# Scores over 64 rows, TensorE operands at multiples of 64 bytes, query weights in quarters of 128 columns

## The chip, the cores and the metric

The kernel runs on one core of one Trainium2 chip. The metric is the device time of one execution in microseconds, as the median of three runs. TensorE is called PE, its load of the stationary operand PEld, VectorE DVE, ScalarE ACT, GpSimd POOL and SyncE SP, as in the profile. "Stationary" is the operand of a matmul that is loaded into the array first, "moving" the one that streams through it.

## What is computed

One transformer block over 2048 tokens of width 576. Attention has 32 query heads of width 18 and one head of keys and values that all of them share; the feed-forward part multiplies two linear branches and has no other nonlinearity.

```python
# x: [1, 2048, 576], H = 32, Dh = 18, F = 4608
q = (ln(x) @ wq), in 32 heads of 18;  k = ln(x) @ wk;  v = ln(x) @ wv
p = softmax(q k^T * 18 ** -0.5)
h = x + (p v, heads side by side) @ wo
g, u = ln(h) @ w_gate, ln(h) @ w_up
out = h + (g * u) @ w_down
```

## The kernel before

**Tiling.** The tokens are worked on in four blocks of 512 (`TB`), the keys in 16 tiles of 128. Attention of a block goes over 8 groups of four heads, over 16 key tiles, and over two pairs of heads. `pair` (L573) does one such step: `scores` (L591) issues two matmuls, one for each head of the pair. One has its operands in partitions 0 and up, the other in partitions 64 and up, so that each uses half of the array's rows. Then ACT takes the exponential of both, 128x1024 values, in one instruction (L594). The operands of a score have 56 rows: 54 of them are 18 query rows in a split of three parts, and rows 54 and 55 hold a bound of the score that is subtracted (the keys' rows there are -1). `flush` and `values` (L596) multiply the exponentials with the values: four matmuls of 32 columns each, in float32, which the trace shows as eight.

**Precision.** Nearly all other matmuls are in the type float32r, and each product of two matrices is done in three passes, high by high, high by low and low by high, with the halves made by a cast and a subtraction (`split`, L86).

**Feed-forward.** `ffn(b)` (L966) goes over 36 slices of 128 hidden columns. A slice is a sweep of 27 steps; each step is a pair of matmuls over 64 rows (L986), one for the gate and one for the up branch, in the two halves of the array, with the normalised tokens `X` moving and the weights `ws` stationary. While attention of a later block is still to be done, a sweep calls `pair` ahead of steps 0, 4, 8, ..., 24 (L983), and the results go to the tiles `pg` and `pu`; in the last block they go to `gu`. Behind every second sweep `down` (L892) multiplies two slices with the down weights: 42 matmuls (L946) of 128 rows, 128 columns and 288 moving columns. There the products of gate and up, which lie in the tile `room` as `A`, are the stationary operand, and the weights `wdo` move. The output projection of attention (`project`, L733, matmuls at L750) has the same shape, with its stationary operand in `oT` or in `o_hl`, a part of `room`.

**Order of the work.** Every engine executes its instructions in the order in which the program issues them, and that order is written out by hand: attention of block 0 first, beside the projections of the queries, then attention of blocks 1 to 3 inside the sweeps of blocks 0 to 2, then the sweeps of block 3 alone. In the opening part (`keys_values`, L134) TensorE projects keys, values and the queries of block 0 (L233, L284), and turns the normalised tokens (L201, L210). The queries of blocks 1 to 3 are projected in `queries` (L436), as pairs of matmuls over 64 rows and 126 columns, seven heads at a time.

**Query tiles.** The tile of a group's queries has two buffers, taken in turn from a pool (L346, L559). Four DMAs on SP's queue fill it (`load_q`, `load_m`): 54 rows and 2 rows for each half. Partitions 56 to 63 and 120 to 127 are not filled. In the keys, `kT`, the partitions 32 to 63 and 96 to 127 are set to -1 once (L163) and then filled up to row 53 of each half.

**Where tiles lie.** Tiles lie one behind the other in the order of the pools, each rounded up to 32 bytes of a partition. With the sizes in the code, `kT`, `V`, the query tiles, the exponentials, `X`, `ws`, `wdo` and the `XT` of the four blocks start at multiples of 64 bytes. The pool `oT`, which holds `x23`, `oT` and `room` one after the other, starts 32 bytes past one. The query weights `wq_h` and `wq_l` have rows of 504 columns (2016 bytes), and a group of seven heads starts every 504 bytes, so that most of their slices start off a multiple of 64.

Of the kernel before, what the change touches and what calls it, by code (L numbers as in the profile page):

```python
# [17 lines left out]
F32 = mybir.dt.float32  # L18
F32R = mybir.dt.float32r
I32 = mybir.dt.int32  # L20
AF = mybir.ActivationFunctionType
ALU = mybir.AluOpType
# [3 lines left out]
P = 128  # L26
S, D, H, DH, F = 2048, 576, 32, 18, 4608
TB = 512
NB = S // TB
NQ = TB // P  # L30
# [24 lines left out]
class Block:  # L55
# [78 lines left out]
    def keys_values(self, others):  # L134

        pe, act, dve, sp, pool = self.pe, self.act, self.dve, self.sp, self.nc.gpsimd
        p0 = self.op
        x01 = [self.hp.tile([P, NQ, D], F32, tag="h", name=f"x{b}") for b in range(2)]
        x23 = self.otp.tile([P, 2, NQ, D], F32, tag="oT", name="x23")
        xs = x01 + [x23[:, 0], x23[:, 1]]  # L140
        self.h.update(enumerate(x01))
        wkr = self.qp.tile([P, 5, 6 * DH], F32, tag="q", name="wkr")
        cols = [(slice(None), slice(None), slice(h0 * DH, (h0 + n) * DH)) for h0, n in QT]
        wqr = [self.qp.tile([P, 5, 7 * DH], F32, tag="q", name="wqr0")]
        wqr += [self.w0.tile([P, 5, 7 * DH], F32, tag="wo_r", bufs=3, name=f"wqr{i}") for i in range(1, 4)]
        for lo, hi in ((0, 1), (1, 2), (2, 4)):
            sp.dma_start(xs[0][:, lo:hi], self.tokens(self.x, 0)[:, lo:hi])
        sp.dma_start(self.C, self.cst)
# [8 lines left out]
        n = 5 * 6 * DH  # L157
# [17 lines left out]

        def scale(lo, hi, eng):
            r = self.rstd(mv[:, lo:hi, 1], f"a{lo}", eng, hi - lo)
            n = self.lp.tile([P, hi - lo], F32, tag=f"n{hi - lo}", name=f"n{lo}")
            if eng is pool:
                pool.tensor_tensor(n, mv[:, lo:hi, 0], r, ALU.mult)  # L180
                pool.tensor_scalar(n, n, -1.0, None, ALU.mult)
            else:
                dve.scalar_tensor_tensor(n, mv[:, lo:hi, 0], -1.0, r, ALU.mult, ALU.mult)
            for j in range(lo, hi):
                rs[j] = r[:, j - lo:j - lo + 1], n[:, j - lo:j - lo + 1]
# [33 lines left out]
        def parts(n=3):  # L219

            for _ in range(n):
                b, r, tr = trs.pop(0)
                XT = self.XT[b]
                if r is None:
                    self.split_tail(XT[:, 8, :], tr)
                else:
                    sl = slice(2 * r * P, (2 * r + 2) * P)
                    self.split(XT[:, 0:4, sl], XT[:, 4:8, sl], tr)

# [43 lines left out]
            dve.tensor_copy(self.V[:, lo:hi, 1:1 + DH], psv[:, :, 44 - DH:44])  # L273

        def highs(i, cast):
            cast(self.wq_h[cols[i]], wqr[i])

        def lows(i):
            pool.tensor_tensor(self.wq_l[cols[i]], wqr[i], f32(self.wq_h[cols[i]]), ALU.subtract)

        def query(i):
            psq = psqs[i] = self.ps_f(f"psq0_{i}")
            for k, (w, m) in enumerate(highs_first(self.wq_h[cols[i]], self.wq_l[cols[i]], self.XT[0])):
                pe.matmul(psq[:7 * DH], w, m, start=(k == 0), stop=(k == 13))  # L284
                yield

# [15 lines left out]
            self.flush(len(self.pend) - 1)  # L302

        q0, q1, q2, q3 = (query(i) for i in range(4))
        warm = self.ps_a("warm")
        for _ in range(WARM):
            pe.transpose(warm[:, 0:P], self.ident, self.ident)
        stats(0, 4)
# [13 lines left out]
        lows(2)  # L322
        stats(6, 8)
        scale(4, 8, pool)
        drain(project(0))
        mean()
        some(q0, 15)
# [15 lines left out]
        apply(1, 2, 3)  # L343
        stats(10, 11)
        some(q1, 6)
        q = self.qt[0, 0] = self.qp.tile([P, 2, TB], F32R, tag="q", name="q0_0")  # L346
        some(k0)
        self.load_q(q, 0, 0)
        self.load_m(q, 0, 0)
# [86 lines left out]
    def queries(self, b):  # L436

        pe, act, dve, sp = self.pe, self.act, self.dve, self.sp
        for i, (h0, n) in enumerate(QT):
            r = n * DH  # L440
            psq, psr = self.ps_f(f"psq{b}_{i}"), self.ps_f(f"psr{b}_{i}")
            w_h, w_l = self.wq_h[:, :, h0 * DH:h0 * DH + r], self.wq_l[:, :, h0 * DH:h0 * DH + r]
            for k, (w, m) in enumerate(passes(w_h, w_l, self.XT[b])):
                for o, ps in ((0, psq), (64, psr)):
                    pe.matmul(ps[:r], w[o:o + 64], m[o:o + 64], start=(k == 0), stop=(k == 13))
                if k < 13:
                    yield 1
                if k == 5 and self.tqs and 0 < self.tqs[0][0] < b:
                    self.bounds(self.tqs[0][0])
            qs = self.qb.tile([P, 2, TB], F32R, tag="qs", bufs=QS, name=f"qs{b}_{i}")  # L450
            t = f32(qs[:r, 0])
            dve.tensor_copy(t, psr[:r])
            src = f32(qs[:r, 1])
            dve.tensor_tensor(src, psq[:r], t, ALU.add)
            self.parts_q(r, qs, src)
            drain(self.store_q(b, h0, n, qs))
            yield 2.5
        self.last_heads(b)
        yield 0
        if b == NB - 1:  # L460
            yield 4
            self.bounds(b)
# [90 lines left out]
    def prefetch_q(self, b, g):  # L553

        if g == NG:
            b, g = b + 1, 0
        if b == NB or (b, g) in self.qt or self.known[b] < 4 * g + 4:
            return
        self.qt[b, g] = q = self.qp.tile([P, 2, TB], F32R, tag="q", name=f"q{b}_{g}")  # L559
        self.load_q(q, b, g)  # L560
        self.load_m(q, b, g)

# [27 lines left out]

    def scores(self, s_, p_, q, t, pr):  # L591
        for i, o in enumerate((0, 64)):
            self.pe.matmul(s_[:, i], self.kT[o:o + 56, t * P:(t + 1) * P], q[o:o + 56, pr], start=True, stop=True)  # L593
        self.act.activation(p_, s_, AF.Exp, scale=SCALE)  # L594

    def values(self, acc, Ps, t):  # L596
# [114 lines left out]

    def load_wo_0(self, c):

        w = self.w0.tile([P, 5, 7 * DH], F32, tag="wo_r", bufs=3, name=f"wo_r{c}")
        r = self.wo_r0[c] = w.rearrange("p a b -> p (a b)")[:, 0:D]
        self.sp.dma_start(r, self.wo0[:, c])

    def split_wo_0(self):
# [437 lines left out]
    def run(self):  # L1156
# [8 lines left out]
        with ExitStack() as st:  # L1165
            pool = lambda name, bufs, **k: st.enter_context(tc.tile_pool(name=name, bufs=bufs, **k))
            cp, self.lp, self.hp = pool("const", 1), pool("ln", 2), pool("resid", 2)
            self.qp, self.pp, self.op, self.otp = pool("q", 2), pool("P", P_BUFS), pool("o", 1), pool("oT", 1)
            self.ps, self.w0 = pool("ps", 1, space=PSUM), pool("w0", 3)
            self.C = cp.tile([P, C_W], F32, name="C")  # L1170
            self.ident = self.C[:, C_ID:C_ID + P]
            self.kT = cp.tile([P, S], F32R, name="kT")
            self.V = cp.tile([P, NT, 32], F32, name="V")
            self.G = cp.tile([P, 64], F32R, name="G")
            self.mx = cp.tile([H, 8], F32, name="mx")
            st.enter_context(tc.manual_schedule())
            with tc.tile_pool(name="p0q", bufs=1) as self.p0q:
                self.wq_h = self.p0q.tile([P, 5, 28 * DH], F32R, name="wq_h")
                self.wq_l = self.p0q.tile([P, 5, 28 * DH], F32R, name="wq_l")
                self.kvq = self.p0q.tile([P, NB, TB], F32, name="kvq")  # L1180
                self.XT = [self.p0q.tile([P, 9, TB], F32R, tag=f"XT{b}", name=f"XT{b}") for b in range(NB)]
                with tc.tile_pool(name="qb", bufs=2) as self.qb:
                    def rest():
                        for b in range(1, NB):
                            yield from self.queries(b)
                    others = rest()
                    self.keys_values(others)
                    self.cast = self.dve.tensor_copy
                    live, due = True, 0.0
                    while live:  # L1190
                        if self.n_pair >= WO_FROM and not self.wo_r0:
                            for c in range(3):
                                self.load_wo_0(c)
                        self.pair()
                        due += RATE
                        while due > 0 and live:
                            z = next(others, None)
                            live = z is not None
                            due -= z or 0
                        self.pair()  # L1200
                        self.run_aux(1)
                        self.flush(len(self.pend) - 1)
            self.wp, self.hh, self.p2 = pool("w", 2), pool("hid", 4), pool("P2", 1)
            self.blocks()
            self.guard()
# [4 lines left out]
P_BUFS = 6  # L1210
# [34 lines left out]
def f32(ap):  # L1245
    return ap.bitcast(F32)
# [10 lines left out]
def highs_first(W, Wl, XT):  # L1257

    p = passes(W, Wl, XT)
    return p[0:12:3] + p[2:12:3] + p[1:12:3] + p[12:]  # L1260
# [7 lines left out]
def drain(gen):  # L1268
    for _ in gen:
        pass  # L1270
# [76 lines left out]
```

## Time and profile before

| | |
|---|---|
| median of 3 runs | 2292.12 us (2291.93 to 2294.34) |
| profiled execution | 2291.9 us |
| its span, first to last instruction | 2290.4 us |
| granted TensorE clock | 0.999 |
| PE busy | 2268.7 us, 99% |
| ACT, DVE, POOL busy | 1436.5, 1180.3, 681.3 us |

The profiled execution took 1.5 us more than its span, and it lies within the range of the runs. Matmuls are pipelined: one starts while the one before it still runs, so the durations in a row of the profile overlap, and the pace of TensorE is read from the distance of starts. In the view in order of time, a row gives the start of a run of like instructions, the time from its start to its end, the engine, the line and what was done, with the count behind the "x".

### The profile page before, as it was taken

The page shows a single profiled execution, that of the slowest core. Times are in us where ns is not written, and L with a number is a line of the kernel's source. Part 1 is how long each engine was busy: PE and PEld are TensorE (multiplying, and loading weights), DVE is VectorE, ACT ScalarE, POOL GpSimd, SP SyncE. Part 2 cuts the span into 40 slices and gives each one's busy share as a digit, 9 for nine tenths or more (in the row PEclk, how much of TensorE's full clock was granted, in tenths as well). Part 3 has the DMA queues.
Part 4 walks back from the last instruction along what each step waited for, and adds up shares of the span by engine and source line. Part 5 has one row for each costly group of instructions (what it writes and reads, how often), then busy time and mean ns, then how long its engine had stood idle before and what let it go on. Part 6 is the DMA issues. An engine that isn't in the chain of part 4 may idle for free.

```text
span 2290.4 us, 45926 instructions
## 1 busy us (share of the span) xinstructions
PE 2268.7 (99%) x18114; PEld 1599.6 (70%) x18114; DVE 1180.3 (52%) x2152; ACT 1436.5 (63%) x1877; POOL 681.3 (30%) x856
## 2 busy tenths in 40 slices
PE   8999999999999999999999999999999999999998
PEld 6333346677777767677767677777767788888987
DVE  8232435565656567343434355444444476566665
ACT  5889887776676666767666767667677623232332
POOL 4000003455554444122221222222122233333342
PEclk9999999999999999999999999999999999999999
DMA  5222304434333344533333343633333354655553
GB/s 176 81 75 73 111 30 136 148 139 151 136 122 128 136 159 137 207 115 122 113 114 105 125 128 125 192 125 120 98 118 118 120 173 171 213 171 171 179 186 109
DMA packets 127129, 306.75 MB, mean 134 GB/s; under 512 B 17553, under 2 KB 17681, under 8 KB 126265
## 3 DMA queue, kind: packets, MB, share of 16 engines
q1 hardware_dynamic: 126905, 303.73, 39.8%
q8 instruction: 145, 2.38, 0.4%
q14 instruction: 79, 0.65, 0.1%
HBM read 233.76 MB, written 55.67 MB: 126 GB/s over the span
## 4 chain that ended last, share of the span: by engine, by line


## 5 line engine op out<-in xcount | busy, mean ns | idle before, releaser
L594 ACT ACTIVATE P<-s 128x1024 f32<-128x1024 f32 x1024 | 1024.0, 1026 | 271.4 <-PE s L593 189.6
L986 PE MATMUL pg<-X,ws 64*128 64x512 f32 x2592 | 706.9, 391 | 0.0
L986 PE MATMUL pu<-X,ws 64*128 64x512 f32 x2592 | 706.7, 391 | 0.1
L986 PEld LDWEIGHTS pg<-X,ws 64*128 64x128 f32 x2592 | 480.2, 186 | 75.9 <-issue 1.2
L986 PEld LDWEIGHTS pu<-X,ws 64*128 64x128 f32 x2592 | 478.1, 186 | 19.1 <-DVE h L751 1.0
L598 PE MATMUL acc<-P,V 128*32 128x512 f32 x4096 | 487.9, 598 | 0.0
L593 PE MATMUL s<-q,kT 56*128 56x512 f32 x2048 | 455.3, 423 | 5.2 <-ACT P L594 3.3
L946 PEld LDWEIGHTS y<-wdo,room 128*128 128x128 f32 x2856 | 386.9, 188 | 46.7 <-issue 44.2
L946 PE MATMUL y<-wdo,room 128*128 128x288 f32 x2856 | 403.7, 300 | 0.0
L953 ACT COPY tmp<-y 128x288 f32<-128x288 f32 x408 | 162.7, 399 | 330.8 <-PE y L946 313.2
L593 PEld LDWEIGHTS s<-q,kT 56*128 56x128 f32 x2048 | 208.1, 184 | 199.4 <-ACT P L594 118.3
L986 PE MATMUL gu<-X,ws 64*128 64x512 f32 x2592 | 301.8, 389 | 0.5 <-DMA X<-X 0.5
L954 POOL TENSOR_TENSOR x<-x,tmp 128x288 f32<-128x288 f32 x204 | 159.1, 810 | 446.2 <-ACT tmp L953 445.7
L598 PEld LDWEIGHTS acc<-P,V 128*32 128x32 f32 x4096 | 114.0, 109 | 242.5 <-issue 231.1
L986 PEld LDWEIGHTS gu<-X,ws 64*128 64x128 f32 x2592 | 247.6, 184 | 48.8 <-issue 4.8
L88 POOL CAST ws<-wr 128x1152 fp32r<-128x1152 f32 x144 | 170.9, 1187 | 325.6 <-PE pu L986 176.2
L954 POOL TENSOR_TENSOR h<-h,tmp 128x288 f32<-128x288 f32 x204 | 159.1, 810 | 345.8 <-ACT tmp L953 345.6
L89 DVE TENSOR_TENSOR ws<-wr,ws 128x1152 fp32r<-128x1152 f32 x144 | 199.1, 1383 | 74.7 <-POOL ws L88 74.7
L1020 DVE TENSOR_TENSOR hf<-pu,g 128x512 f32<-128x512 f32 x96 | 66.3, 691 | 269.0 <-ACT g L1016 265.6
L949 DVE TENSOR_TENSOR x<-x,y 128x288 f32<-128x288 f32 x272 | 117.7, 452 | 145.6 <-PE y L946 145.6
L949 DVE TENSOR_TENSOR h<-h,y 128x288 f32<-128x288 f32 x272 | 118.4, 454 | 111.8 <-PE y L946 109.8
L89 DVE TENSOR_TENSOR room<-S,room 128x1024 fp32r<-128x1024 f32 x68 | 85.1, 1251 | 147.7 <-ACT room L88 147.7
(172 smaller groups left out, 1621.9 us busy)
## 6 DMA issues: line engine op xcount, KB each, us to landing
wdo<-wd_dram SPq DMA_DIRECT2D x369, 288.0 KB
wr<-in_wgu_dram SPq DMA_DIRECT2D x144, 576.0 KB
wd_dram<-wdo SPq DMA_DIRECT2D x123, 288.0 KB
q<-q_dram SPq DMA_DIRECT2D x64, 216.0 KB
raw<-in_wd_dram SPq DMA_DIRECT2D x36, 288.0 KB
q_dram<-qs SPq DMA_DIRECT2D x15, 504.0 KB
X<-X SPq DMA_DIRECT2D x24, 256.0 KB
ob<-ob SPq DMA_DIRECT2D x121, 36.0 KB
```

Source lines behind the costliest of these rows:

```text
L88: (copy or self.cast)(hi, src)
L89: self.dve.tensor_tensor(lo, src, f32(hi), ALU.subtract)
L593: self.pe.matmul(s_[:, i], self.kT[o:o + 56, t * P:(t + 1) * P], q[o:o + 56, pr], start=True, stop=True)
L594: self.act.activation(p_, s_, AF.Exp, scale=SCALE)
L598: self.pe.matmul(acc[32 * j:32 * j + 32, :], self.V[:, t, :], Ps[j // 2][:, j % 2, :], start=(t == 0), stop=(t == NT - 1), skip_group_chec ...
L946: pe.matmul(y[:, :HD], m[:, t * P:(t + 1) * P], k, start=(first and j == 0), stop=(j == 2), skip_group_check=True)
L949: dve.tensor_tensor(hs, hs, y[:, :HD], ALU.add)
L953: act.copy(z, y[:, :HD])
L954: pool.tensor_tensor(hs, hs, z, ALU.add)
L986: pe.matmul(ps, w[o:o + 64, wk, c], X[o:o + 64, xk, c], start=(j == 0), stop=(j == 26))
L1020: dve.tensor_tensor(hf, pu, g, ALU.mult)
```

## The change

Three things are changed together.

1. **Scores.** Both operands of a score now have 64 rows. Rows 56 to 63 of the keys are -1 already; the queries' rows there must be zero. So there are two query tiles for the whole kernel, `self.q2`, set to zero once by POOL and used in turn, in place of tiles that are taken from the pool for each group.
2. **Places.** A tile of 8 floats, `gap`, goes ahead of `oT` in its pool, and smaller tiles change their size or place (the scale tile `n`, and the raw query weights `wqr`, which now lie where `XT3` comes later), so that `oT`, `room` and what lies behind them start at multiples of 64 bytes. `XT3` is made when it is first written.
3. **Query weights.** `wq_h` and `wq_l` are kept as four quarters of 128 columns, of which 126 are used, so that each slice starts at a multiple of 64 bytes.

The scratch of TensorE's opening transposes (`warm`) moves to another PSUM tile.

```diff
@@ keys_values
+        self.otp.tile([P, 8], F32, tag="gap", name="gap")
         x23 = self.otp.tile([P, 2, NQ, D], F32, tag="oT", name="x23")
-        wkr = self.qp.tile([P, 5, 6 * DH], F32, tag="q", name="wkr")
+        wkr = self.qp.tile([P, 5, 6 * DH], F32, tag="q0", name="wkr")
-        wqr = [self.qp.tile([P, 5, 7 * DH], F32, tag="q", name="wqr0")]
-        wqr += [self.w0.tile([P, 5, 7 * DH], F32, tag="wo_r", bufs=3, name=f"wqr{i}") for i in range(1, 4)]
+        wqr = [self.qp.tile([P, 5, 7 * DH], F32, tag="q1", name="wqr0")]
+        late = self.p0q.tile([P, 3, 5, 7 * DH], F32, tag="XT3", name="wqr")
+        wqr += [late[:, i] for i in range(3)]
...
-            n = self.lp.tile([P, hi - lo], F32, tag=f"n{hi - lo}", name=f"n{lo}")
+            n = self.lp.tile([P, NQ], F32, tag="n", name=f"n{lo}")[:, :hi - lo]
...
+                if b == len(self.XT):
+                    self.XT.append(self.p0q.tile([P, 9, TB], F32R, tag=f"XT{b}", name=f"XT{b}"))
...
-            cast(self.wq_h[cols[i]], wqr[i])
+            cast(self.wq_h[:, :, i, :7 * DH], wqr[i])
...
-        warm = self.ps_a("warm")
+        warm = self.ps_m("warm")
...
         scale(4, 8, pool)
+        self.q2 = [self.qp.tile([P, 2, TB], F32R, tag=f"q{i}", name=f"q{i}") for i in range(2)]
+        for q in self.q2:
+            pool.memset(f32(q), 0.0)
...
-        q = self.qt[0, 0] = self.qp.tile([P, 2, TB], F32R, tag="q", name="q0_0")
+        q = self.qt[0, 0] = self.q2[0]
@@ queries
-            w_h, w_l = self.wq_h[:, :, h0 * DH:h0 * DH + r], self.wq_l[:, :, h0 * DH:h0 * DH + r]
+            w_h, w_l = self.wq_h[:, :, i, :r], self.wq_l[:, :, i, :r]
@@ prefetch_q
-        self.qt[b, g] = q = self.qp.tile([P, 2, TB], F32R, tag="q", name=f"q{b}_{g}")
+        self.qt[b, g] = q = self.q2[g % 2]
@@ scores
-            self.pe.matmul(s_[:, i], self.kT[o:o + 56, t * P:(t + 1) * P], q[o:o + 56, pr], start=True, stop=True)
+            self.pe.matmul(s_[:, i], self.kT[o:o + 64, t * P:(t + 1) * P], q[o:o + 64, pr], start=True, stop=True)
@@ load_wo_0
-        w = self.w0.tile([P, 5, 7 * DH], F32, tag="wo_r", bufs=3, name=f"wo_r{c}")
-        r = self.wo_r0[c] = w.rearrange("p a b -> p (a b)")[:, 0:D]
+        r = self.wo_r0[c] = self.w0.tile([P, D], F32, tag="wo_r", bufs=3, name=f"wo_r{c}")
@@ run
-                self.wq_h = self.p0q.tile([P, 5, 28 * DH], F32R, name="wq_h")
-                self.wq_l = self.p0q.tile([P, 5, 28 * DH], F32R, name="wq_l")
+                self.wq_h = self.p0q.tile([P, 5, 4, P], F32R, name="wq_h")
+                self.wq_l = self.p0q.tile([P, 5, 4, P], F32R, name="wq_l")
-                self.XT = [... for b in range(NB)]
+                self.XT = [... for b in range(NB - 1)]
```

The code of the lows (`wq_l`) and of `query` is changed as that of the highs. The number, shape and order of the matmuls and of the exponentials stay, but for the 64 rows.

More of the change, by code (lines that the diff above doesn't have):

```diff
@@ L275, in highs @@
         def highs(i, cast):
-            cast(self.wq_h[cols[i]], wqr[i])
+            cast(self.wq_h[:, :, i, :7 * DH], wqr[i])
         def lows(i):
-            pool.tensor_tensor(self.wq_l[cols[i]], wqr[i], f32(self.wq_h[cols[i]]), ALU.subtract)
+            pool.tensor_tensor(self.wq_l[:, :, i, :7 * DH], wqr[i], f32(self.wq_h[:, :, i, :7 * DH]), ALU.subtract)
         def query(i):
             psq = psqs[i] = self.ps_f(f"psq0_{i}")
-            for k, (w, m) in enumerate(highs_first(self.wq_h[cols[i]], self.wq_l[cols[i]], self.XT[0])):
+            for k, (w, m) in enumerate(highs_first(self.wq_h[:, :, i, :7 * DH], self.wq_l[:, :, i, :7 * DH], self.XT[0])):
                 pe.matmul(psq[:7 * DH], w, m, start=(k == 0), stop=(k == 13))
@@ L1167, in run @@
             cp, self.lp, self.hp = pool("const", 1), pool("ln", 2), pool("resid", 2)
-            self.qp, self.pp, self.op, self.otp = pool("q", 2), pool("P", P_BUFS), pool("o", 1), pool("oT", 1)
+            self.qp, self.pp, self.op, self.otp = pool("q", 1), pool("P", P_BUFS), pool("o", 1), pool("oT", 1)
             self.ps, self.w0 = pool("ps", 1, space=PSUM), pool("w0", 3)
@@ L1177, in run @@
             with tc.tile_pool(name="p0q", bufs=1) as self.p0q:
-                self.wq_h = self.p0q.tile([P, 5, 28 * DH], F32R, name="wq_h")
-                self.wq_l = self.p0q.tile([P, 5, 28 * DH], F32R, name="wq_l")
+                self.wq_h = self.p0q.tile([P, 5, 4, P], F32R, name="wq_h")
+                self.wq_l = self.p0q.tile([P, 5, 4, P], F32R, name="wq_l")
                 self.kvq = self.p0q.tile([P, NB, TB], F32, name="kvq")
-                self.XT = [self.p0q.tile([P, 9, TB], F32R, tag=f"XT{b}", name=f"XT{b}") for b in range(NB)]
+                self.XT = [self.p0q.tile([P, 9, TB], F32R, tag=f"XT{b}", name=f"XT{b}") for b in range(NB - 1)]
                 with tc.tile_pool(name="qb", bufs=2) as self.qb:
```

## The prediction, made before the changed kernel was run

> **What bounds the kernel now.** I read the page first: busy time per engine, the slices and the costliest groups.
>
> ```profile
> PE 2268.7 (99%) x18114; PEld 1599.6 (70%) x18114; DVE 1180.3 (52%) x2152; ACT 1436.5 (63%) x1877; POOL 681.3 (30%) x856
> ...
> PE   8999999999999999999999999999999999999998
> ...
> PEclk9999999999999999999999999999999999999999
> ...
> L594 ACT ACTIVATE P<-s 128x1024 f32<-128x1024 f32 x1024 | 1024.0, 1026 | 271.4 <-PE s L593 189.6
> L986 PE MATMUL pg<-X,ws 64*128 64x512 f32 x2592 | 706.9, 391 | 0.0
> ...
> L598 PE MATMUL acc<-P,V 128*32 128x512 f32 x4096 | 487.9, 598 | 0.0
> L593 PE MATMUL s<-q,kT 56*128 56x512 f32 x2048 | 455.3, 423 | 5.2 <-ACT P L594 3.3
> L946 PEld LDWEIGHTS y<-wdo,room 128*128 128x128 f32 x2856 | 386.9, 188 | 46.7 <-issue 44.2
> L946 PE MATMUL y<-wdo,room 128*128 128x288 f32 x2856 | 403.7, 300 | 0.0
> ...
> L593 PEld LDWEIGHTS s<-q,kT 56*128 56x128 f32 x2048 | 208.1, 184 | 199.4 <-ACT P L594 118.3
> L986 PE MATMUL gu<-X,ws 64*128 64x512 f32 x2592 | 301.8, 389 | 0.5 <-DMA X<-X 0.5
> ...
> L986 PEld LDWEIGHTS gu<-X,ws 64*128 64x128 f32 x2592 | 247.6, 184 | 48.8 <-issue 4.8
> ```
>
> PE is busy in every slice at the full clock, and none of its large groups has more than 5.2 us of idle time ahead of it. ACT waits for PE (189.6 us ahead of the exponentials), not the other way round. Next I read the waits of PE, longest first, and one stretch of the windows:
>
> ```profile
> PE warm L307 <- DMA C<-in_cst_dram: 6.3, 1, 6.3
> PE s L593 <- ACT P L594: 3.3, 11, 0.4
> ```
>
> ```profile
> 1000.00:1100.00 100.00, 100.00 (x834) 70.92 (x836) 43.40 (x75) 72.64 (x92) 21.35 (x25) 1.00 0.37 120
> ```
>
> Of all waits, 6.3 us are the first load and 3.3 us are for ACT. So the time is the sum of TensorE's paces, and ACT (72.64 us of 100 in a stretch with attention) has room for a faster TensorE. A busy PE hides its pace; the view in order of time shows it. First the last block, without scores:
>
> ```profile
> 1998.74 9.23 PE L986 MATMUL gu<-X,ws 64*128 64x512 f32 x80
> 2007.90 5.92 PE L946 MATMUL y<-wdo,room 128*128 128x288 f32 x42
> ```
>
> Of a run, the last matmul's own duration is taken off. The 40 gate-up pairs go at (9.23 - 0.389) / 39 = 0.2267 us a pair, the 42 down matmuls at (5.92 - 0.300) / 41 = 0.1371 us each, waits between their stages included. Then a sweep with scores, in the same view (the rows of the other half of the array left out):
>
> ```profile
> 1818.71 0.40 PE L593 MATMUL s<-q,kT 56*128 56x512 f32 x2
> 1818.95 0.39 PE L986 MATMUL pg<-X,ws 64*128 64x512 f32 x1
> ...
> 1819.18 0.39 PE L986 MATMUL pg<-X,ws 64*128 64x512 f32 x1
> ...
> 1819.41 0.39 PE L986 MATMUL pg<-X,ws 64*128 64x512 f32 x1
> ...
> 1819.64 0.39 PE L986 MATMUL pg<-X,ws 64*128 64x512 f32 x1
> ...
> 1819.87 0.40 PE L593 MATMUL s<-q,kT 56*128 56x512 f32 x2
> ...
> 1821.03 0.40 PE L593 MATMUL s<-q,kT 56*128 56x512 f32 x2
> ```
>
> A score pair and four gate-up pairs take 1.16 us, twice (1818.71 to 1819.87 to 1821.03). Five pairs at the pace of the last block would take 5 x 0.2267 = 1.134 us. The starts are 0.24, 0.23, 0.23, 0.23 and 0.23 apart: slowest behind the score, and the next ones a little slow as well. So **a score inside a sweep costs about 0.026 us more than a gate-up pair**, though it has the same moving columns. What differs is the 56 rows.
>
> **Part 1, 64 rows.** It adds no instruction and takes none away. If the 56 rows cause the 0.026 us, a score becomes like a gate-up pair. A sweep of blocks 0 to 2 has seven scores among its steps, and 93 sweeps have them (2592 / 27 = 96 sweeps write `pg`, and the last sweep of each of the three blocks has none): 93 x 7 = 651 scores, 651 x 0.026 = 16.9 us. The first of each sweep comes behind a change of array shape, which has its own price, so I take 16 us. The bounds are 0 (the rows are not the cause) and 16.9. Scores in block 0 alternate with matmuls of another shape, and I give them nothing. ACT doesn't take it back: an exponential lasts 1.026 us, and a score would come every 1.134 us.
>
> The Trainium skill's page "TensorE: Matmul & The Clock Gate", section "LDWEIGHTS (loading the stationary operand)", speaks against this part: the load of weights follows their columns, and a load over 32 rows takes as long as one over 128. The trace agrees for the load itself, 184 ns in the score's row and in that of `gu`; by that rule alone the sum would be 0.
>
> **The new query tiles** cost two memsets of 1024 columns on POOL and no DMA. POOL and SP at that place, in order of time:
>
> ```profile
> 1.49 3.65 POOL L163 MEMSET kT<- 32x2048 f32 x2
> ```
>
> ```profile
> 24.12 0.73 POOL L181 TENSOR_SCALAR n<-n 128x4 f32<-128x4 f32 x1
> 29.47 0.19 POOL L113 TENSOR_SCALAR va<-mv 128x4 f32<-128x4 f32 x1 [4.62 <-DVE mv L104]
> ```
>
> ```profile
> 28.37 0.76 SPq L517 DMA_DIRECT2D q<-q_dram x2
> ```
>
> ```profile
> 35.79 0.74 PE L593 MATMUL s<-q,kT 56*128 56x512 f32 x4
> ```
>
> At 3.65 / 4096 = 0.9 ns a column they take some 0.9 us each and end near 26.7, inside POOL's idle 4.62 us, ahead of the first load of queries at 28.37 on SP's queue, which the first score at 35.79 waits for. I cost them at nothing; without that cover the first score would start up to 1.8 us later. A later load still goes to the tile that the group before last has read, so its wait is the old one, and SP's order stays.
>
> **Part 2, the stationary operand of the down and output matmuls**, moves from 32 bytes past a multiple of 64 onto one. The same stationary load, misaligned and not, stands in the opening transposes: those of block 0 read the tile `xh` at a multiple of 64 bytes, those of block 3 read `x23`, 32 past one.
>
> ```profile
> 11.22 1.91 PE L201 MATMUL tr<-C,xh 128*128 128x128 f32 x16
> 12.97 1.04 PE L210 MATMUL trt<-C,xh 128*128 128x128 f32 x8
> ```
>
> ```profile
> 48.57 1.94 PE L201 MATMUL tr<-C,x 128*128 128x128 f32 x16
> 50.34 0.49 PE L210 MATMUL trt<-C,x 128*128 128x128 f32 x3
> ```
>
> Sixteen take 1.91 us and 1.94 us: 2 ns each at most. Transposes are float32 and down matmuls float32r, so this is near, not the same. Other bounds: by columns, the aligned gate-up pace gives 0.2267 x 288 / 512 = 0.1275 us, so a down matmul could gain up to 0.1371 - 0.1275 = 9.6 ns. A loss is bounded by the slowest float32r pace of the trace, the key projection, one in four of whose stationary slices lies at a multiple of 64:
>
> ```profile
> 45.07 3.51 PE L233 MATMUL psk<-XT,wk 128*108 128x512 f32 x14
> ```
>
> ```profile
> L233 PE MATMUL psk<-XT,wk 128*108 128x512 f32 x56 | 13.9, 399 | 0.5 <-ACT XT L88 0.5
> L750 PE MATMUL yo<-wos,room 128*128 128x288 f32 x336 | 50.4, 304 | 0.9 <-DVE x L751 0.8
> L445 PE MATMUL psq<-XT,wq_h 64*126 64x512 f32 x108 | 39.2, 395 | 0.0
> ```
>
> It goes at (3.51 - 0.399) / 13 = 0.2393 us, 12.6 ns over a gate-up pair, or 7 ns for 288 columns. With 2856 down matmuls and 336 of the output projection (3192; a few hundred in smaller groups left out) the part lies between -31 us (9.6 ns) and +22 us (7 ns). I take 0, by the transposes.
>
> The Trainium skill's page "SBUF — State Buffer", section "Specifications (TRN2)", gives lines of 16 bytes; a start at 32 bytes past 64 is on such a line already, so by it this part would bring 0 too. No row here shows a line's size.
>
> **Part 3, the query weights**: 12 groups of 14 pairs by the code (108 of them with the high weights, as the row says), 168 in all. Their loads keep 126 columns. If each lost all 12.6 ns of the key projection's excess, it would be 168 x 0.0126 = 2 us. I take 0, and the moved raw weights and scratch as 0, since they keep their instructions.
>
> **The sum.** 2291.9 (the profiled execution, 2290.4 of span and 1.5 around it) - 16 + 0 + 0 = 2275.9 us. Against the median of 2292.12 it is the same within 0.2: **2276 us**, 0.7% faster.
>
> **The rivals.** *The rows don't matter* (no change): the score's 0.026 us come from something that stays, such as its wait for ACT, its semaphore or its place between two accumulations. For it speaks the equal load of 184 ns, and the page above; against it, that gate-up pairs also carry waits and signals and keep 0.2267 in the last block. It gives 2292, from 2288 to 2296.
>
> *The aligned stationary operand is faster too*: down matmuls lose 2 to 9.6 ns, 6 to 31 us, with the scores' gain or in its place. For it: the down matmul is the one large group off the 64 bytes. Against it: the transposes. It gives 2245 to 2270, about 2260.
>
> *Aligned operands collide* (slower): once stationary `room` and moving `wdo` both start on multiples of 64 bytes, the load and the stream of a down matmul ask for the same place of the memory at once and one waits. The price is up to 7 ns x 3192 = 22 us: 2276 + 22 = 2298 beside the scores' gain, 2314 without it. It decides from 16 / 3192 = 5 ns a matmul. Against it: `X` and `ws` are both aligned and go at the steady 0.2267.
>
> **How the numbers follow.** Forecast (2270 to 2287) 0.45; the aligned operand faster too 0.17; no change 0.26; collision 0.12. So faster by over 0.2% has 0.62, within 0.2% (4.6 us, about what a measurement of this kernel can tell from no change) 0.26, slower 0.12. The range takes in the forecast, no change and the nearer half of the second: 2254 to 2296.
>
> **What would show it.** In the changed profile a score and four gate-up pairs should take 1.134 us instead of 1.16; if they keep 1.16, part 1 failed. Forty-two down matmuls should still take about 5.9 us; 5.5 would show the second case, over 6.1 the third. The opening should reach its first score at the same time, near 35.8 us. The prediction is wrong if the pace of any large group changes that I left alone, above all the 0.2267 of the last block.

## The result and the profile after

The changed kernel took 2289.86 us (median of 20 runs, 2288.39 to 2291.01), the kernel before 2293.43 us beside it (20 runs). The ratio is 0.9987, with a 95% interval of 0.9981 to 0.9993: faster by 3 to 4 us, within the 0.2% that counted as no change, and not by the 16 us of the forecast. The profiled execution has a span of 2287.7 us.

The page of the changed kernel, the lines that answer to those of before (engine, line and operation, operands and shapes, count, then busy us, mean ns of one, and the idle time ahead):

```profile
PE 2264.9 (99%) x18114; PEld 1596.8 (70%) x18114; DVE 1182.4 (52%) x2152; ACT 1436.9 (63%) x1877; POOL 684.4 (30%) x858
...
L601 ACT ACTIVATE P<-s 128x1024 f32<-128x1024 f32 x1024 | 1024.4, 1027 | 266.8 <-PE s L600 188.2
L992 PE MATMUL pg<-X,ws 64*128 64x512 f32 x2592 | 704.9, 390 | 0.0
...
L600 PE MATMUL s<-q,kT 64*128 64x512 f32 x2048 | 453.8, 422 | 5.2 <-ACT P L601 3.1
...
L952 PE MATMUL y<-wdo,room 128*128 128x288 f32 x2856 | 403.9, 300 | 0.1
...
L600 PEld LDWEIGHTS s<-q,kT 64*128 64x128 f32 x2048 | 207.9, 184 | 199.7 <-ACT P L601 118.4
```

The score now has 64 rows, and the page shows little of it: PE's busy time is 3.8 us shorter, and no row tells where, since the busy times of overlapping matmuls hide the pace, before as after. The view in order of time shows it. First TensorE of the changed kernel, four scores of a sweep (the gate-up pairs between them left out) and a group of down matmuls of the last block:

```profile
1815.36 0.40 PE L600 MATMUL s<-q,kT 64*128 64x512 f32 x2
...
1816.51 0.40 PE L600 MATMUL s<-q,kT 64*128 64x512 f32 x2
...
1817.67 0.40 PE L600 MATMUL s<-q,kT 64*128 64x512 f32 x2
...
1818.82 0.40 PE L600 MATMUL s<-q,kT 64*128 64x512 f32 x2
```

```profile
2005.38 5.93 PE L952 MATMUL y<-wdo,room 128*128 128x288 f32 x42
```

A score and four gate-up pairs take 1.153 us (3.46 / 3), where 1.16 was before and 1.134 was forecast. The down matmuls take 5.93 us, as before (5.92). So in the steady part of a sweep about a quarter of the extra cost of a score is gone, and the down matmuls have not moved. Over all distances of this kind in the trace (start of a score to the start of the next in the same half of the array with four gate-up matmuls between, 1124 of them in each kernel) the median went from 1.164 to 1.154 us and the mean from 1.190 to 1.185. By the traces 94 sweeps have seven scores (the prediction counted 93): 658 scores at 5 ns are 3.3 us. The time from the first sweep to the first one of the last block fell by as much, from 1466.5 to 1463.2 us.

POOL and SP at the place of the new memsets, then TensorE's first instructions and its first scores:

```profile
26.01 1.84 POOL L331 MEMSET q<- 128x1024 f32 x2
```

```profile
29.58 0.36 SPq L524 DMA_DIRECT2D q<-q_dram  x1
```

```profile
7.59 5.05 PE L311 MATMUL warm<-C 128*128 128x128 f32 x24 [7.59 <-DMA C<-in_cst_dram]
```

```profile
37.52 0.73 PE L600 MATMUL s<-q,kT 64*128 64x512 f32 x4
```

The memsets take 0.92 us each and end at 27.85, ahead of the load of the queries, as forecast. But the first score starts at 37.52 us and not at 35.79. Of these 1.73 us, 1.31 stand ahead of everything on TensorE: its first instruction waited 7.59 us for the constants, 6.28 before. The other 0.42 us have no run of their own; a price of the memsets within that is not excluded.

### The profile page after: what moved, and what is told of

Read it like the earlier page. It is cut to its first block, busy times and chain, and to the rows that moved or that the text cites. A ratio compares the mean times of both kernels' runs of the same rounds, so it can differ in the third digit from the quotient of the medians.

```text
span 2287.7 us, 45951 instructions
## 1 busy us (share of the span) xinstructions
PE 2264.9 (99%) x18114; PEld 1596.8 (70%) x18114; DVE 1182.4 (52%) x2152; ACT 1436.9 (63%) x1877; POOL 684.4 (30%) x858
## 4 chain that ended last, share of the span: by engine, by line
PE 95%; DVE 2%; DMA 1%; ACT 1%; issue 0%; SPq 0%; DVEq 0%; ACTq 0%
PE acc L605 20%; PE y L952 17%; PE pg L992 14%; PE gu L992 13%; PE s L600 12%; PE pu L992 12%; PE yo L756 3%; PE psq L452 2%; PE y L910 1%; ACT P L601 1%; DMA x<-in_x_dram 0%; DMA X<-X 0%; DMA q_dram<-qs 0%; DVE XT L89 0%; PE ye L910 0%
## 5 line engine op out<-in xcount | busy, mean ns | idle before, releaser
L600 PE MATMUL s<-q,kT 64*128 64x512 f32 x2048 | 453.8, 422 | 5.2 <-ACT P L601 3.1
L600 PEld LDWEIGHTS s<-q,kT 64*128 64x128 f32 x2048 | 207.9, 184 | 199.7 <-ACT P L601 118.4
```

The costliest lines, as they stand in the source:

```text
L600: self.pe.matmul(s_[:, i], self.kT[o:o + 64, t * P:(t + 1) * P], q[o:o + 64, pr], start=True, stop=True)
```

## The experiments

At the start there were two theories. **R**: the 64 rows bring the gain, and what remains of a score's extra cost is something that the change does not touch (the wait for ACT, ACT's reads of PSUM, the place in the stream). **P**: the gain comes from the places of the tiles, and the rows do nothing. A third came up after the first four runs. In what follows "the distance" is the one defined above, a score and four gate-up pairs, 1.134 us if all five go at the pace of a gate-up pair.

### e1_rows and e2_places: one part at a time

`e1_rows` is the kernel before with part 1 alone, `e2_places` the changed kernel without it:

```diff
 # e2_places, against the changed kernel
-    self.kT[o:o + 64, t * P:(t + 1) * P], q[o:o + 64, pr]
+    self.kT[o:o + 56, t * P:(t + 1) * P], q[o:o + 56, pr]
```

> The kernel before with part 1 alone: scores over 64 rows, two fixed query tiles. The whole change gained 0.13% (about 3 us of the 16 that were forecast for this part). Theory R (the 64 rows bring that gain, and nothing else does): ratio to before 0.998 to 0.9993, a score and four gate-up pairs take about 1.155 us instead of 1.160. Theory P (the places bring it): ratio 1.000 within 0.0004 and 1.160 us as before.

> The changed kernel with scores over 56 rows again: parts 2 and 3 alone. Theory R: ratio to before 1.000 within 0.0004. Theory P: 0.9987. If the aligned down matmuls gained and something else took it back, the 42 down matmuls take under 5.85 us and another group is slower.

Rows alone: 0.9976 (0.9965 to 0.9986), median distance 1.156 us. Places alone: 1.0002 (0.9993 to 1.0012), median distance 1.160. So the gain is that of the rows, and parts 2 and 3 bring nothing by themselves; theory R had said 0.998 to 0.9993 for the rows, a little less than they brought. The rows alone have a mean distance of 1.183 us, the whole change 1.185; that the places took something back is likely, but the two intervals overlap.

### e3_probe: what in a score costs

The last block has no scores, and its gate-up pairs keep a steady pace. Extra pairs were put into its sweeps, in nine cases of four sweeps each, with their results in unused PSUM tiles:

```diff
+                    if b == NB - 1 and self.first and j and j % 4 == 0:
+                        self.probe(f // 4, w, X)
...
+            rows = 56 if case == 1 else 64
+            pa, pm = self.ps_a("pa"), self.ps_m("pm")
+            for o, ps in ((0, pa), (64, pm)):
+                if case == 3:
+                    self.pe.matmul(ps, w[o:o + 64, 0, 0], X[o:o + 64, 0, 0], start=True, stop=True)
+                else:
+                    self.pe.matmul(ps[:n], kT[o:o + rows, c:c + n], q[o:o + rows, 0], start=True, stop=True)
```

> The changed kernel with extra work in the 36 sweeps of the last block, ahead of steps 4, 8, ... 24, four sweeps to a case: 0 nothing, 1 a score pair over 56 rows, 2 over 64 rows, 3 a further pair with the gate-up operands, 4 the score pair with its stationary operand moved by 32 bytes, 5 by 16 bytes, 6 with 126 columns, 7 over 64 rows with the exponentials of its result, 8 only exponentials of constant data. The results of the extra work are not used. If the rows cause the extra cost of a score, case 1 takes about 1.160 us for a score and four pairs and case 2 takes 1.134 (five pairs of 0.2267). If interleaving another operand does, cases 1 and 2 both take 1.15 to 1.16 and case 3 1.134. If the exponentials do, only case 7 (and 8, if it is their memory traffic) goes over 1.14. If a misaligned stationary operand costs, cases 4 and 5 are over case 2 by 0.005 or more.

The view in order of time has, for one sweep of a case, the first and the last of its six extra pairs in one half of the array. Cases 1, 2 and 3:

```profile
1995.96 0.39 PE L1059 MATMUL pm<-q,kT 56*128 56x512 f32 x1
...
2001.76 0.39 PE L1059 MATMUL pm<-q,kT 56*128 56x512 f32 x1
```

```profile
2038.59 0.39 PE L1059 MATMUL pm<-q,kT 64*128 64x512 f32 x1
...
2044.36 0.39 PE L1059 MATMUL pm<-q,kT 64*128 64x512 f32 x1
```

```profile
2080.98 0.39 PE L1057 MATMUL pm<-X,ws 64*128 64x512 f32 x1
...
2086.66 0.39 PE L1057 MATMUL pm<-X,ws 64*128 64x512 f32 x1
```

A fifth of each stretch is the distance: 5.80 / 5 = 1.160 us with 56 rows, 5.77 / 5 = 1.154 with 64 rows, 5.68 / 5 = 1.136 with the gate-up operands themselves. The medians over the 40 distances of a case are 1.160, 1.153 and 1.133. The other cases, by the same medians: 4 (stationary operand moved by 32 bytes) 1.158, 5 (by 16 bytes) 1.160, 6 (126 columns) 1.162, 8 (exponentials alone; four gate-up pairs and a fifth by their pace) 1.134. Cases 4 and 5 are 5 and 7 ns over case 2; the probe does not tell whether that is a start off a multiple of 64 or only another place. Case 7, with exponentials of the result, went over 1.3 because both extra tiles have one buffer and wait for ACT; it says nothing.

So a score's 26 ns need no exponential and no wait: they are there in a bare stream. With keys and queries where they lie here, 7 ns of them belong to the 56 rows, and the other 19 to something in which keys and queries differ from the gate-up operands. The place in the stream is not it, since case 3 stands at the same place.

### e4_noread: no wait for the exponentials

```diff
-        self.act.activation(p_, s_, AF.Exp, scale=SCALE)
+        self.act.activation(p_.rearrange("p a (c q) -> p (a c) q", q=256),
+                            self.C[:, 0:256].unsqueeze(1).broadcast_to([P, 4, 256]), AF.Exp, scale=SCALE)
```

> The changed kernel with the exponentials taken of constant data in place of the scores: the scores are computed and not read, so a score waits for no exponential and ACT reads no PSUM for it. If the scores' wait for ACT or ACT's reads of PSUM cause the extra cost of a score, a score and four gate-up pairs take 1.134 us; if they don't, about 1.155 as in the changed kernel.

The median distance is 1.153 us, as in the changed kernel: ACT's reads of PSUM and the scores' wait for ACT do not make the 19 ns. The upper quartile fell from 1.163 to 1.154, and the time was 2277.58 us (one run): there are waits for ACT too, beside the 19 ns. With case 3, theory R's account of the remainder is refuted; P was refuted by `e2_places`.

### e5_phase and e6_match: where the operands start

What differs between the operands of case 3 and those of case 2 is the tile. In the program's allocation, gate-up weights and tokens start at the same place within 256 bytes; in the changed kernel the keys start 192 bytes and the queries 64 bytes past it (256 bytes are taken as one turn; in the kernel before it is 0 and 192). That gave **theory A**: two neighbours in TensorE's stream go at full pace when their operands start at the same place within some number of bytes. `e5_phase` reads two copies of the tokens at chosen starts, `e6_match` moves keys and queries in the whole kernel:

```diff
 # e6_match, against the changed kernel
+            cp.tile([P, 16], F32, name="gap_k")                      # ahead of kT
+        self.qp.tile([P, 32], F32, tag="gap_q", name="gap_q")       # ahead of the query tiles
-        self.otp.tile([P, 8], F32, tag="gap", name="gap")
+        self.otp.tile([P, 88], F32, tag="gap", name="gap")
```

> The changed kernel with an extra pair of 64 rows, 128 and 512 columns ahead of steps 4, 8, ... 24 of the last block's sweeps, three sweeps to a case; its result is not used. The operands are two copies of the normalised tokens, read at chosen starts within 512 bytes, counted from the start of the gate-up operands, which lie at the same place within 512 bytes as each other: (stationary, moving) = 0 (0, 0), 1 (320, 0), 2 (0, 320), 3 (320, 320), 4 (64, 0), 5 (128, 0), 6 (256, 0), 7 (0, 64), 8 (0, 128), 9 (0, 256), 10 (the keys' tile, 0), 11 (0, the query tile). Theory A (the place within 512 bytes relative to the neighbours sets the extra cost): case 0 takes 1.134 us for the pair and four gate-up pairs, the others more, up to 1.153 as the keys and queries did. Theory B (it is the tile or its contents, whatever its start): case 0 takes 1.15 too. Theory C (one operand alone does it): cases 10 and 11 differ, one at 1.134 and one at 1.15.

> The changed kernel with three gaps between tiles, so that keys, queries, gate-up weights and tokens all start at the same place within 512 bytes (448); nothing else is changed. Theory A: a score and four gate-up pairs fall from 1.153 us to 1.134, 651 x 0.019 = 12 us off the changed kernel, ratio to before about 0.993. Theory B or C: as the changed kernel, 0.9987.

The first and last extra pair of one sweep of `e5_phase`, in cases 0 (same place), 1 (stationary 320 bytes off) and 6 (stationary 256 off):

```profile
1959.15 0.39 PE L1061 MATMUL pm<-T,T 64*128 64x512 f32 x1
...
1964.82 0.39 PE L1061 MATMUL pm<-T,T 64*128 64x512 f32 x1
```

```profile
1987.77 0.39 PE L1061 MATMUL pm<-T,T 64*128 64x512 f32 x1
...
1993.53 0.39 PE L1061 MATMUL pm<-T,T 64*128 64x512 f32 x1
```

```profile
2150.34 0.39 PE L1061 MATMUL pm<-T,T 64*128 64x512 f32 x1
...
2156.02 0.39 PE L1061 MATMUL pm<-T,T 64*128 64x512 f32 x1
```

They give 1.134, 1.152 and 1.136 us. The medians of all cases (30 distances each):

| stationary off by | moving off by | distance, us |
|---|---|---|
| 0 | 0 | 1.133 |
| 64 | 0 | 1.153 |
| 128 | 0 | 1.147 |
| 256 | 0 | 1.133 |
| 320 | 0 | 1.153 |
| 0 | 64 | 1.154 |
| 0 | 128 | 1.140 |
| 0 | 256 | 1.134 |
| 0 | 320 | 1.154 |
| 320 | 320 | 1.168 |
| keys (192) | 0 | 1.153 |
| 0 | queries (64) | 1.160 |

In these cases what counts is the start within 256 bytes, relative to the neighbours: 256 is as good as 0, and 320 as bad as 64, so the 512 bytes of theory A were too many. Either operand can cost, and reads of the same tile are fast or slow by their start. Theories B and C are refuted. In the whole kernel it holds as well; four scores of a sweep in `e6_match`:

```profile
1808.70 0.39 PE L601 MATMUL s<-q,kT 64*128 64x512 f32 x2
...
1809.84 0.39 PE L601 MATMUL s<-q,kT 64*128 64x512 f32 x2
...
1810.97 0.39 PE L601 MATMUL s<-q,kT 64*128 64x512 f32 x2
...
1812.11 0.39 PE L601 MATMUL s<-q,kT 64*128 64x512 f32 x2
```

Three distances take 3.41 us, 1.137 each; the median is 1.134. The time was 2285.2 us, ratio 0.9965 (0.9951 to 0.9978). That is 5 us below the changed kernel and not the 12 that were expected.

### e7_match56, e8_down and e9_match_noread

`e7_match56` is `e6_match` with 56 rows. `e8_down` gives the down weights rows of 320 columns, so that both halves start at the place of the down matmuls' stationary operand. `e9_match_noread` is `e6_match` with the exponentials of constant data, as in `e4_noread`; attention's result is then not that of the scores.

```diff
 # e8_down, in load_wd and right
-        self.wp.tile([P, 2, HD], F32R, tag="wdo", ...)
+        self.wp.tile([P, 2, 320], F32R, tag="wdo", ...)[:, :, :HD]
```

> The kernel of e6_match with scores over 56 rows. If the rows cost by themselves, as 7 ns in cases 1 and 2 of e3_probe, a score and four gate-up pairs take a median of 1.141 us or more against 1.134, and the ratio to before is about 0.9985. If the rows cost only where the places differ, 1.134 us and 0.9965 as e6_match.

> The kernel of e6_match with each half of a down-weight tile at a row of 320 columns in place of 288 (1280 bytes), so that both halves start at the same place within 256 bytes as the stationary operand of the down matmuls; 288 columns are used as before. If the places set the pace of the down matmuls too, 42 of them take less than 5.85 us and the ratio to before falls below 0.995. If their pace is set by something else (their 288 columns and the waits between their stages), 5.9 us and 0.9965 as e6_match.

> The kernel of e6_match with the exponentials taken of constant data in place of the scores, as in e4_noread: a score waits for no exponential. e6_match had a median of 1.134 us for a score and four gate-up pairs, but a quarter of them took over 1.17. If that quarter is a wait for ACT, it goes here: the upper quartile falls to 1.14 and the time to about 2277.6 - 12 = 2266 us. If it is something else on TensorE, the upper quartile stays near 1.17 and the time near 2272.

**56 rows at equal places** are as slow as ever: ratio 1.0005 (0.9996 to 1.0014), median distance 1.160 us. Four scores of its trace:

```profile
1816.72 0.40 PE L601 MATMUL s<-q,kT 56*128 56x512 f32 x2
...
1817.88 0.40 PE L601 MATMUL s<-q,kT 56*128 56x512 f32 x2
...
1819.04 0.40 PE L601 MATMUL s<-q,kT 56*128 56x512 f32 x2
...
1820.20 0.40 PE L601 MATMUL s<-q,kT 56*128 56x512 f32 x2
```

So the distance with 56 rows was 1.160 at both sets of places, 1.134 needs 64 rows and equal places together, and 64 rows alone get to 1.153 to 1.156. The first expectation had the distance right (1.141 or more) and the ratio wrong (0.9985), the second missed: the rows' price is 26 ns at equal places and 7 at unequal ones.

**The down matmuls** did not react: 42 of them took a median of 5.91 us in the last block (5.92 in `e6_match` and before), and the ratio is 0.9963 (0.995 to 0.9977), the same as `e6_match`.

**Without the wait for ACT** the time was 2268.21 us (one run), 17 us below `e6_match`: 6.7 us of it ahead of the first sweep, 9.4 in the sweeps. The upper quartile of the distance fell from 1.173 to 1.138 us, as expected, but most of the slow distances stayed. A sweep has seven scores and six distances, and their means by place in the sweep (94 sweeps, from the starts in the traces) tell which ones wait:

| distance in the sweep | before | the change | `e6_match` | `e9_match_noread` |
|---|---|---|---|---|
| first | 1.278 | 1.275 | 1.281 | 1.283 |
| second to fourth | 1.160 | 1.152 | 1.135 | 1.135 |
| fifth | 1.164 | 1.157 | 1.153 | 1.137 |
| sixth | 1.226 | 1.232 | 1.230 | 1.159 |

The first is slow in every kernel, with rows and places as they may be; no run here tells by what. The sixth distance goes over 1.2 us in every second sweep, 47 of 94, before the change already, and in 2 of 94 without the wait. Of these 47 sweeps 45 have a conversion on ACT among their exponentials, the sums for the down matmuls, and no other sweep has it. ACT in such a sweep of `e6_match`, and the weight load of its sixth score, which waits:

```profile
659.73 3.31 ACT L602 ACTIVATE P<-s 128x1024 f32<-128x1024 f32 x3 [1.48 <-PE s L601]
662.94 1.04 ACT L88 CAST room<-S 128x1024 fp32r<-128x1024 f32 x1
663.88 3.86 ACT L602 ACTIVATE P<-s 128x1024 f32<-128x1024 f32 x4
```

```profile
664.96 0.18 PEld L601 LDWEIGHTS s<-q,kT 64*128 64x128 f32 x2 [0.29 <-ACT P L602]
```

The conversion of 1.04 us stands between the third and the fourth exponential. The fourth starts at 663.88, 0.8 us after its score has ended, and ends near 664.91. Scores have two PSUM tiles in turn, so the sixth score needs the tile of the fourth, and its weights are loaded at 664.96. What that costs shows in the distance behind it. The wait stands in the row of the weight load and hardly in that of the matmul. From 360 to 1800 us, which holds nearly all sweeps, it came to this before and in `e6_match`:

```profile
PEld s L593 <- ACT P L594: 10.5, 45, 0.4
```

```profile
PEld s L601 <- ACT P L602: 13.8, 47, 0.4
```

From the first sweep to the first one of the last block, the changed kernel took 1463.2 us, `e6_match` 1457.0, `e4_noread` 1457.3 and `e9_match_noread` 1447.6 (starts of the first `pg` and `gu` in the traces). Equal places save 9.7 us where nothing waits for ACT, and 6.2 us where scores do: the faster the stream, the longer scores wait for their exponentials, and 3.5 us go back (one trace each).

### e10_rows_match: rows and equal places, and nothing else

```diff
 # against e1_rows
+        self.otp.tile([P, 48], F32, tag="gap", name="gap")
+        self.qp.tile([P, 16], F32, tag="gap_q", name="gap_q")
```

> The kernel of e1_rows (before, with part 1 alone) with two gaps that bring the queries to the same place within 256 bytes as the keys, the gate-up weights and the tokens (128); the down matmuls' stationary operand stays 32 bytes past a multiple of 64 and the query weights stay as before. If 64 rows and equal places are all that it takes, a score and four gate-up pairs take a median of 1.134 us and the ratio to before is that of e6_match, 0.9965. If multiples of 64 bytes for the other operands have a part in it, it stays between that and the 0.9976 of e1_rows.

It took 2284.55 us, ratio 0.996 (0.9946 to 0.9974), with a median distance of 1.134 us. The stationary operand of the down matmuls is still 32 bytes off a multiple of 64, and the query weights are as before. So of the change, part 1 is of use and parts 2 and 3 are not, and for the whole gain part 1 needs two gaps that the change does not have. This kernel is faster than the one before and than the change by intervals that do not touch; `e6_match` and `e8_down` can't be told from it.

All comparisons with an interval:

| kernel | rows | keys, queries off by | median (mean) distance, us | ratio to before |
|---|---|---|---|---|
| before | 56 | 0, 192 | 1.164 (1.190) | 1 |
| e2_places | 56 | 192, 64 | 1.160 (1.190) | 1.0002 (0.9993 to 1.0012) |
| e7_match56 | 56 | 0, 0 | 1.160 (1.190) | 1.0005 (0.9996 to 1.0014) |
| the change | 64 | 192, 64 | 1.154 (1.185) | 0.9987 (0.9981 to 0.9993) |
| e1_rows | 64 | 0, 192 | 1.156 (1.183) | 0.9976 (0.9965 to 0.9986) |
| e6_match | 64 | 0, 0 | 1.134 (1.176) | 0.9965 (0.9951 to 0.9978) |
| e8_down | 64 | 0, 0 | 1.134 (1.177) | 0.9963 (0.995 to 0.9977) |
| e10_rows_match | 64 | 0, 0 | 1.134 (1.176) | 0.996 (0.9946 to 0.9974) |

## Why the prediction was wrong

**What bounds the kernel** was right: TensorE's pace. A score inside a sweep did cost 26 ns more than a gate-up pair, and wherever some of that was taken away the time fell.

**The step that failed** is the first of part 1: "What differs is the 56 rows", and with it "If the 56 rows cause the 0.026 us, a score becomes like a gate-up pair". The rows were read as the only difference because they were the only one that the profile prints. The other one, the start of the tiles within 256 bytes, stands in the program's allocation and was looked at for multiples of 64 only. With it unequal, the rows bring 7 ns in the bare stream, not 26, and 3 to 4 us in place of 16; with it equal they bring all 26, and a score does become like a gate-up pair, 1.134 us. No row of the profile told the two apart; a score with other operands in the steady last block did.

**A second step failed as well**: "ACT doesn't take it back". The exponential lasts 1.027 us as assumed, but ACT does more than exponentials: in every second sweep a conversion of 1.04 us stands among them, and the sixth score waits. The prediction read 3.3 us of waits for ACT in the row of the matmul, and showed without a word the row of the weight load, `199.4 <-ACT P L594 118.3`; 10.5 us of that are in the sweeps. And the first distance of a sweep did not change at all, where 0.9 us were taken off for it. So even with rows and equal places, 9.4 us of the forecast 16 came in the sweeps (1466.5 to 1457.0 us in `e10_rows_match`): the second to fourth distances gained their 25 ns, the fifth 11, the first and the sixth none. Of what equal places save in the sweeps, 3.5 of 9.7 us went back to the wait.

**The rival "the rows don't matter"** named the right range for the time, 2288 to 2296, by luck: waits, signals and the place in the stream do not make the 26 ns (case 3, `e4_noread`), and the rows do matter. Here the Trainium skill's page "TensorE: Matmul & The Clock Gate", section "LDWEIGHTS (loading the stationary operand)", was right on the load, 184 ns with 56 and with 64 rows. The zero that the prediction drew from it did not hold: the distance went from 1.160 to 1.134 us by the rows at equal places.

**Parts 2 and 3** were costed at nothing, and that held: 1.0002 for the two together, 5.93 us against 5.92 for the down matmuls; part 3 has no run of its own. The collision that was feared did not come, neither there nor in `e8_down`. **The memsets** took 0.92 us each against 0.9 and ended ahead of the load that they had to precede. That the first score would start at 35.8 us did not hold (37.52), most of it by a later first load.

What stays open is the mechanism: why a difference of 64 to 192 bytes between the starts of neighbouring operands, or 56 rows instead of 64, costs TensorE 7 to 35 ns in a pair and its four neighbours. The runs show when it happens and not what in the chip does it. The Trainium skill's page "SBUF — State Buffer", section "Specifications (TRN2)", gives lines of 16 bytes. By such lines alone all starts at multiples of 64 would be alike; in the probe a start 64 bytes off took 1.153 us against 1.133, so something else is at work, and the measurement decides.

## What to carry to other kernels

Where matmuls of different operands alternate on a full TensorE, read the distance of starts in the view in order of time against a stretch of one kind alone, since busy times and mean durations hide a loss of 2%. If the mixture is slower, try full rows (64 in place of 56 here) together with equal starts of the operands within 256 bytes: rows without equal starts gave a third to 60% of the gain in time (0.9987 and 0.9976 against 0.996), equal starts without rows gave nothing (1.0005). A slow instruction that differs in several ways from its fast neighbour wants an experiment for each of them before a price is put on one. And before an engine is said to keep up, look for its other work in the same stretch: a mean of 72.64 us of 100 hid a conversion in every second sweep.

## What the runs showed of the hardware

- The pace of a gate-up pair was 0.227 us with all starts at 128 bytes within 256 (before) and with all at 192 (the changed kernel), and a score and four pairs took 1.134 us with all at 192 (`e6_match`) and with all at 128 (`e10_rows_match`): it is the difference between neighbours that costs, not the place itself.
- A stationary operand of 126 columns cost about as much as 56 rows, at the same unequal starts: 1.162 and 1.160 us against 1.153 in the probe.
- Down matmuls did not react to their starts, although the two halves of their moving operand start 128 bytes apart (within 256) in all kernels but `e8_down`: 5.92 us for 42 before and 5.91 in `e8_down`.
- A pair whose own two operands start alike, but both 320 bytes off their neighbours', was the slowest of the probe: 1.168 us.
- Exponentials of constant data beside the stream (case 8) cost TensorE nothing: 1.134 us.
- A score's wait for an exponential stands in the row of its weight load, 13.8 us in 47 waits in the sweeps of `e6_match`; the matmul's row has 3.1 us in the whole run.
